# A retention layer and a gated MLP on one core: from scheduled program order to a fixed one, with attention output made transposed and its state kept in PSUM

## The chip, the core and the metric

The kernel runs on one core of a Trainium2 chip. The metric is device time in microseconds (us), as the median of several runs of the whole kernel. Each run also has a span (first to last instruction of the core) and a mean granted clock of TensorE. The engines are named as in the profile: PE (TensorE matmuls), PEld (its weight loads), DVE (VectorE), ACT (ScalarE), POOL (GpSimd) and SP (SyncE, which here issues DMA).

## The reference, cut to what matters

```python
B, H, S, D = 4, 8, 768, 64            # q, k, v: fp32, N(0, 0.1)
for t in range(S):                    # retention: a decaying state per head
    state = gamma * state + outer(k[t], v[t])
    y[t]  = scale * q[t] @ state
x = y as [3072 tokens, 512]
h = x @ w_in                          # w_in  [512, 2048]
g = h * cos(h)
out = g @ w_out                       # w_out [2048, 512]
```

Both kernels compute the recurrence in chunks of 128 tokens (24 chunks, 6 per batch): inside a chunk as masked attention with decay factors folded into q and k (or v), between chunks through the state. The MLP runs on groups of four chunks (512 tokens, six groups). For each group there are 16 "F steps" (four matmuls of 512 columns into one bank, then a sine on ACT and a multiply on DVE) and 64 "O matmuls" for the output. F(g,f) is F step f of group g. Everything that PE reads is bf16, so both weight matrices are cast from fp32 once.

## The kernel before

The parts that the change touches. x is made with tokens on partitions, so each group needs 16 transposes by PE and four DVE copies before its F steps ("T"). The state is summed in fp32 in SBUF by DVE. The program is written chunk by chunk, with MLP units put in by a table.

```python
def load_weights():
    for i in range(KIN):
        ...                                        # whole rows of w_in, 1 MB each
        nc.vector.tensor_copy(out=w_in_sb[:, i, :], in_=st)
    for i in range(KOUT):
        ...
        nc.scalar.copy(out=w_out_sb[:, i, :], in_=st[:, :DM])    # on ACT

def moe_tr_unit(g, i):
    for j in range(GT):
        nc.tensor.transpose(pt[:, ts(j, 128)], x_sb[:, (g * GT + j) % XR, ts(i, 128)], ident)
    nc.vector.tensor_copy(out=xt[:, i, :], in_=pt)

def moe_f_unit(g, f):
    for i in range(KIN):
        nc.tensor.matmul(hp, lhsT=w_in_sb[:, i, ts(f, 128)], rhs=xt[:, i, :], ...)
    nc.scalar.activation(out=cosb, in_=hp, func=AF.Sin, bias=halfpi)
    nc.vector.tensor_tensor(out=gt[:, f, :], in0=hp, in1=cosb, op=ALU.mult)
...
def conv_qk(cc):                                   # decay factors, both on DVE
    nc.vector.tensor_tensor(out=qg[:, co + cc], in0=qf[cc][0], in1=gqbig[:, co + cc], op=ALU.mult)
    nc.vector.tensor_tensor(out=kg[:, co + cc], in0=qf[cc][1], in1=gkbig[:, co + cc], op=ALU.mult)
...
for j in range(2):                                 # state: fp32 add, then a scaled bf16 copy
    nc.vector.tensor_tensor(out=stt[...], in0=stt[...], in1=dps[j][...], op=ALU.add)
for j in range(2):
    nc.vector.tensor_scalar(out=stb[...], in0=stt[...], scalar1=float(scale), ...)
```

Of the kernel before, what the change touches and what calls it, by code (L numbers as in the profile page):

```python
# [13 lines left out]
ALU = mybir.AluOpType  # L14


@with_exitstack
def kernel(
# [9 lines left out]
    nc = tc.nc  # L28
# [6 lines left out]
    NCH = NC // 2  # L35

    scale = 1.0 / math.sqrt(D)
    gammas = [1.0 - 2.0 ** (-5.0 - h) for h in range(H)]

# [5 lines left out]
    XR = 12  # L45

    const = ctx.enter_context(tc.tile_pool(name="const", bufs=1))
    wpool = ctx.enter_context(tc.tile_pool(name="wpool", bufs=1))
    xpool = ctx.enter_context(tc.tile_pool(name="xpool", bufs=1))

    ident = const.tile([128, 128], BF16)
    maskJ = const.tile([128, HP, 128], BF16)
    gqbig = const.tile([128, NC, H, D], BF16)
    gkbig = const.tile([128, NC, H, D], BF16)
    pidx1 = const.tile([128, 1], FP32)
    pidxC = const.tile([128, NC], FP32)
    pidxCn = const.tile([128, NC], FP32)
    halfpi = const.tile([128, 1], FP32)
    def setup_consts_first():
        nc.gpsimd.iota(pidx1, pattern=[[0, 1]], base=1, channel_multiplier=1,  # L60
                       allow_small_or_imprecise_dtypes=True)
        make_identity(nc, ident)

    def setup_consts_early():
        lgbig = wstage.tile([128, 4, H, D], FP32, name="sti")[:, 0]
        for h in range(H):
            nc.vector.memset(lgbig[:, h], math.log(gammas[h]))
        for c in range(NC):
            nc.vector.tensor_scalar(out=pidxC[:, c : c + 1], in0=pidx1,
                                    scalar1=float(128 * c), scalar2=None,  # L70
                                    op0=ALU.add)
        nc.vector.tensor_scalar(out=pidxCn, in0=pidxC, scalar1=-1.0,
                                scalar2=None, op0=ALU.mult)
        for c in range(NC):
            nc.scalar.activation(out=gqbig[:, c], in_=lgbig, func=AF.Exp,
                                 scale=pidxC[:, c : c + 1])
            nc.scalar.activation(out=gkbig[:, c], in_=lgbig, func=AF.Exp,
                                 scale=pidxCn[:, c : c + 1])

    def setup_consts_late():  # L80
        nc.vector.memset(maskJ, float(scale))
        for hp in range(HP):
            nc.gpsimd.affine_select(
                out=maskJ[:, hp], in_=maskJ[:, hp], compare_op=ALU.is_ge,
                fill=0.0, base=0, pattern=[[1, 128]], channel_multiplier=-1,
            )
        nc.gpsimd.memset(halfpi, math.pi / 2.0)

    w_in_sb = wpool.tile([128, KIN, DF], BF16)
    w_out_sb = wpool.tile([128, KOUT, DM], BF16)  # L90
    wstage = ctx.enter_context(tc.tile_pool(name="wstage", bufs=2))

    def load_weights():
        for i in range(KIN):
            st = wstage.tile([128, DF], FP32, name="sti")
            nc.sync.dma_start(out=st, in_=moe_w_in[ts(i, 128), :])  # L96
            nc.vector.tensor_copy(out=w_in_sb[:, i, :], in_=st)
        for i in range(KOUT):
            st = wstage.tile([128, DF], FP32, name="sti")
            nc.sync.dma_start(out=st[:, :DM], in_=moe_w_out[ts(i, 128), :])  # L100
            nc.scalar.copy(out=w_out_sb[:, i, :], in_=st[:, :DM])  # L101

    x_sb = xpool.tile([128, XR, DM], BF16)

    qkv_pool = ctx.enter_context(tc.tile_pool(name="qkv", bufs=2))
    cvt_pool = ctx.enter_context(tc.tile_pool(name="cvt", bufs=2))
    st_pool = ctx.enter_context(tc.tile_pool(name="state", bufs=2))
    tr_pool = ctx.enter_context(tc.tile_pool(name="tr", bufs=2))
    am_pool = ctx.enter_context(tc.tile_pool(name="am", bufs=4))
    xt_pool = ctx.enter_context(tc.tile_pool(name="xt", bufs=2))  # L110
    g_pool = ctx.enter_context(tc.tile_pool(name="g", bufs=2))
    c_pool = ctx.enter_context(tc.tile_pool(name="c", bufs=3))
    o_pool = ctx.enter_context(tc.tile_pool(name="o", bufs=3))

    ps_tr = ctx.enter_context(tc.tile_pool(name="ps_tr", bufs=2, space=bass.MemoryType.PSUM))
    ps_a = ctx.enter_context(tc.tile_pool(name="ps_a", bufs=2, space=bass.MemoryType.PSUM))
    ps_y = ctx.enter_context(tc.tile_pool(name="ps_y", bufs=2, space=bass.MemoryType.PSUM))
    ps_h = ctx.enter_context(tc.tile_pool(name="ps_h", bufs=2, space=bass.MemoryType.PSUM))

    moe_state = {}  # L120

    def moe_tr_unit(g, i):
        if i == 0:
            moe_state["xt", g] = xt_pool.tile([128, KIN, GT * 128], BF16, name="xt")
        xt = moe_state["xt", g]
        pt = ps_tr.tile([128, GT * 128], BF16, name="pt", tag="tr")
        for j in range(GT):
            nc.tensor.transpose(pt[:, ts(j, 128)],
                                x_sb[:, (g * GT + j) % XR, ts(i, 128)], ident)
        nc.vector.tensor_copy(out=xt[:, i, :], in_=pt)  # L130

    def moe_f_unit(g, f):
        if f == 0:
            moe_state["gt", g] = g_pool.tile([128, KOUT, GT * 128], BF16, name="gt")
        xt = moe_state["xt", g]
        gt = moe_state["gt", g]
        hp = ps_h.tile([128, GT * 128], FP32, name="hp")
        for i in range(KIN):
            nc.tensor.matmul(hp, lhsT=w_in_sb[:, i, ts(f, 128)],  # L139
                             rhs=xt[:, i, :],  # L140
                             start=(i == 0), stop=(i == KIN - 1))
        cosb = c_pool.tile([128, GT * 128], BF16, name="cosb")
        nc.scalar.activation(out=cosb, in_=hp, func=AF.Sin, bias=halfpi)  # L143
        nc.vector.tensor_tensor(out=gt[:, f, :], in0=hp, in1=cosb, op=ALU.mult)  # L144

    def moe_o_unit(g, j):
        gt = moe_state["gt", g]
        op = ps_y.tile([128, DM], FP32, name="op", tag="yo")
        for f in range(KOUT):
            nc.tensor.matmul(op, lhsT=gt[:, f, ts(j, 128)],  # L150
                             rhs=w_out_sb[:, f, :],
                             start=(f == 0), stop=(f == KOUT - 1))
        ob = o_pool.tile([128, DM], FP32, name="ob")
        nc.scalar.copy(out=ob, in_=op)  # L154
        nc.gpsimd.dma_start(out=out[ds((g * GT + j) * 128, 128), :], in_=ob)  # L155

    def moe_units_for_group(g):
        for i in range(KIN):
            yield ("T", g, i)
        for f in range(KOUT):  # L160
            yield ("F", g, f)
        for j in range(GT):
            yield ("O", g, j)

    sched = [[] for _ in range(B * NC + 8)]
    for g in range(NG):
        counts = [6, 6, 6, 6] if g < 2 else [4, 4, 4, 4, 2, 2, 2, 2]
        units = list(moe_units_for_group(g))
        pos = 0
        for off, cnt in enumerate(counts):  # L170
            for u in units[pos : pos + cnt]:
                sched[GT * g + 4 + off].append(u)
            pos += cnt
    sched0 = [[] for _ in sched]
    last_t = {}
    for ci, lst in enumerate(sched):
        for u in lst:
            if u[0] == "T":
                last_t[u[1]] = ci
    for ci, lst in enumerate(sched):  # L180
        f = [u for u in lst if u[0] == "F" and last_t[u[1]] < ci][:2]
        sched0[ci] = f
        sched[ci] = [u for u in lst if u not in f]

    def emit_moe0(ci):
        for kind, g, idx in sched0[ci]:
            moe_f_unit(g, idx)

    def emit_moe(ci):
        for kind, g, idx in sched[ci]:  # L190
            if kind == "T":
                moe_tr_unit(g, idx)
            elif kind == "F":
                moe_f_unit(g, idx)
            else:
                moe_o_unit(g, idx)

    def stage_qkv(b, half, v_on_sync=False):
        res = []
        for cc in range(NCH):  # L200
            qf = qkv_pool.tile([128, H, D], FP32, name=f"qf{cc}")
            kf = qkv_pool.tile([128, H, D], FP32, name=f"kf{cc}")
            vf = qkv_pool.tile([128, H, D], FP32, name=f"vf{cc}")
# [9 lines left out]
        return res  # L213

    setup_consts_first()
    pending = [stage_qkv(0, 0, True), stage_qkv(0, 1, True)]
    setup_consts_early()
    setup_consts_late()

# [140 lines left out]
```

## Time and profile before

| | before |
|---|---|
| median of 4 runs | 283.88 us (283.24 to 285.16) |
| span of the profiled run | 278.8 us |
| PE busy | 241.5 us, so PE idle 37.3 us |

First the page of the kernel before. Each digit of the slice rows is the busy share, in tenths, of a fortieth of the span; PEclk is the granted TensorE clock in tenths of full speed. In the last two lines the columns are source line, engine, operation, output and inputs, shapes, count, busy time and mean ns, and then the engine's idle time just before these instructions, with what ended most of it.

```profile
span 278.8 us, 4341 instructions
...
PE 241.5 (87%) x1680; PEld 125.8 (45%) x1680; DVE 167.9 (60%) x324; ACT 143.8 (52%) x222; POOL 55.3 (20%) x82
...
PE   0178868869857999998999999999999999999992
...
PEclk9999999988988999999999999999999999999998
DMA  7999998998997600011000000101001010001011
...
L139 PE MATMUL hp<-xt,w_in_sb 128*128 128x512 bf16 x384 | 100.1, 387 | 4.6 <-DVE gt L144 4.1
...
L150 PE MATMUL op<-w_out_sb,gt 128*128 128x512 bf16 x384 | 90.2, 380 | 5.9 <-ACT w_out_sb L101 5.8
```

The 387 and 380 ns are spans of matmuls that overlap; they are not the rate. For the rate one takes the chain of work that ended last (start, length, what):

```profile
89.81 6.99 PE op L150 x32
```

By the timeline these 32 O matmuls began at 89.73 and ended 7.07 us later. The last one's own span is about 0.38 us, so the 31 steps between starts are (7.07 - 0.38) / 31 = 0.216 us each. The 768 matmuls of F and O at 216 ns are 166 us, the floor of any version that keeps this work at this rate.

The windows view of the same kernel gives busy time by stage (from:to, length, busy us and count of each engine, granted clock, DMA share, GB/s):

```profile
0.00:41.00 41.00, 22.74 (x201) 16.50 (x202) 29.03 (x68) 23.22 (x35) 21.05 (x34) 1.00 1.03 311
41.00:89.00 48.00, 36.74 (x230) 18.19 (x230) 37.35 (x67) 28.67 (x47) 19.83 (x22) 0.93 0.96 290
...
100.00:275.00 175.00, 170.99 (x1172) 85.45 (x1170) 98.41 (x186) 86.42 (x132) 11.33 (x21) 1.00 0.07 29
```

There are two stages. To 89 us the loads bound the kernel (DMA share near 1). From 100 us PE is busy 171 of 175 us and bounds it. The view of waits says what PE stood for (us in total, times, longest):

```profile
PE pq L228 <- DVE qg L248: 14.4, 4, 9.3
PE op L150 <- ACT w_out_sb L101: 5.8, 5, 1.9
```

### The profile page before, as it was taken

The numbers are of one execution on the slowest core, as the hardware profiler recorded it, in microseconds if no ns is written. First come the engines' busy times: TensorE is split into PE (matmuls) and PEld (weight loads), VectorE is DVE, ScalarE is ACT, GpSimd is POOL, SyncE is SP. The second block draws the span as 40 slices with busy tenths as digits, with TensorE's granted clock in tenths as the row PEclk, the third lists the DMA queues.
The fourth block names the chain that finished last, engine by engine and source line by source line (L and its number), as shares of the span: only waits on it lengthen the run. The fifth ranks groups of instructions, "written<-read, shape, count | busy, mean of one in ns | idle before, by whom it ended". The sixth has DMA issues, their size and how long they took to land.

```text
span 278.8 us, 4341 instructions
## 1 busy us (share of the span) xinstructions
PE 241.5 (87%) x1680; PEld 125.8 (45%) x1680; DVE 167.9 (60%) x324; ACT 143.8 (52%) x222; POOL 55.3 (20%) x82
## 2 busy tenths in 40 slices
PE   0178868869857999998999999999999999999992
PEld 0166544434323555444645554545554454444440
DVE  5478799868875179970899873518871345331300
ACT  5964615877544276744376682615753345343410
POOL 8576204542632200011000000000001000001010
PEclk9999999988988999999999999999999999999998
DMA  7999998998997600011000000101001010001011
GB/s 194 330 304 331 394 317 237 299 327 260 319 320 217 190 38 4 0 65 76 12 2 1 2 0 38 40 38 40 1 2 75 0 75 2 38 39 75 2 75 75
DMA packets 39381, 33.84 MB, mean 121 GB/s; under 512 B 32576, under 2 KB 32576, under 8 KB 38848
## 3 DMA queue, kind: packets, MB, share of 16 engines
q1 hardware_dynamic: 34080, 16.26, 20.7%
q0 software_dynamic: 5280, 17.31, 17.5%
q8 instruction: 13, 0.21, 0.3%
q14 instruction: 8, 0.07, 0.1%
HBM read 27.26 MB, written 6.29 MB: 120 GB/s over the span
## 4 chain that ended last, share of the span: by engine, by line
issue 55%; DMA 16%; PE 12%; SPq 5%; POOL 4%; ACT 3%; DVE 3%; POOLq 0%; DVEq 0%; ACTq 0%
DMA sti<-in_moe_w_out_dram 10%; PE hp L139 5%; DMA sti<-in_moe_w_in_dram 4%; POOL out_dram L155 4%; PE op L150 3%; SPq L207 2%; DMA kf_147<-in_k_dram 2%; ACT w_out_sb L101 2%; SPq L210 2%; SPq L96 1%; ACT cosb L143 1%; DVE stb L321 1%; PE pq L228 1%; PE ap L272 1%; ACT sq L231 1%
## 5 line engine op out<-in xcount | busy, mean ns | idle before, releaser
L139 PE MATMUL hp<-xt,w_in_sb 128*128 128x512 bf16 x384 | 100.1, 387 | 4.6 <-DVE gt L144 4.1
L144 DVE TENSOR_TENSOR gt<-hp,cosb 128x512 bf16<-128x512 f32 x96 | 65.5, 687 | 62.8 <-ACT cosb L143 62.0
L150 PE MATMUL op<-w_out_sb,gt 128*128 128x512 bf16 x384 | 90.2, 380 | 5.9 <-ACT w_out_sb L101 5.8
L143 ACT ACTIVATE cosb<-hp,halfpi 128x512 bf16<-128x512 f32 x96 | 65.5, 689 | 39.2 <-PE hp L139 37.5
L150 PEld LDWEIGHTS <-gt 128*128 128x128 bf16 x384 | 36.8, 98 | 48.8 <-issue 6.5
L139 PEld LDWEIGHTS <-w_in_sb 128*128 128x128 bf16 x384 | 35.7, 99 | 42.8 <-issue 11.4
L155 POOL DMA_DIRECT2D out_dram<-ob x24 | 13.0, 542 | 156.8 <-ACT ob L154 156.8
L154 ACT COPY ob<-op 128x512 f32<-128x512 f32 x24 | 14.0, 586 | 53.7 <-PE op L150 53.7
L276 DVE TENSOR_TENSOR amt<-ap,maskJ 128x512 bf16<-128x512 f32 x48 | 32.0, 683 | 9.3 <-PE ap L272 9.0
L231 ACT COPY sq<-pq 128x1024 bf16<-128x1024 bf16 x24 | 24.1, 1011 | 13.1 <-PE pq L229 7.1
L228 PE MATMUL pq<-ident,qg 128*128 128x128 bf16 x96 | 17.3, 245 | 14.4 <-DVE qg L248 14.4
L272 PE MATMUL ap<-sq 64*128 64x128 bf16 x192 | 17.7, 240 | 3.7 <-DVE stt L317 1.8
L297 PE MATMUL yp<-vb,amt 128*128 128x64 bf16 x192 | 19.1, 205 | 1.9 <-DVE amt L276 1.7
L228 PEld LDWEIGHTS <-qg 128*128 128x128 bf16 x96 | 10.3, 110 | 18.2 <-DVE qg L248 15.6
L317 DVE TENSOR_TENSOR stt<-stt,dp 64x256 f32<-64x256 f32 x40 | 16.6, 416 | 2.8 <-PE dp L310 1.7
L297 PEld LDWEIGHTS <-amt 128*128 128x128 bf16 x192 | 14.4, 105 | 7.9 <-DVE amt L276 4.0
L301 ACT CAST x_sb<-yp 128x512 bf16<-128x512 f32 x24 | 14.0, 584 | 7.2 <-PE yp L297 7.2
L229 PE MATMUL pq<-ident,kg 128*128 128x128 bf16 x96 | 17.2, 245 | 0.0
L272 PEld LDWEIGHTS <-sq 64*128 64x128 bf16 x192 | 9.9, 102 | 14.3 <-issue 9.6
L101 ACT CAST w_out_sb<-sti 128x512 bf16<-128x512 f32 x16 | 9.9, 617 | 12.7 <-DMA sti<-in_moe_w_out_dram 12.6
L321 DVE TENSOR_SCALAR stb<-stt 64x256 bf16<-64x256 f32 x40 | 12.2, 306 | 6.8 <-PE yp L290 5.8
L290 PE MATMUL yp<-stb,sq 128*128 128x128 bf16 x80 | 14.8, 236 | 0.5 <-DVE stb L321 0.2
(141 smaller groups left out, 179.7 us busy)
## 6 DMA issues: line engine op xcount, KB each, us to landing
out_dram<-ob POOLq DMA_DIRECT2D x24, 256.0 KB, 2.3
sti<-in_moe_w_in_dram SPq DMA_DIRECT2D x4, 1024.0 KB, 8.8
sti<-in_moe_w_out_dram SPq DMA_DIRECT2D x16, 256.0 KB, 4.1
kf_123<-in_k_dram SPq DMA_DIRECT2D x1, 256.0 KB, 2.7
vf_124<-in_v_dram SPq DMA_DIRECT2D x1, 256.0 KB, 3.4
qf_122<-in_q_dram POOLq DMA_DIRECT2D x1, 256.0 KB, 4.4
kf_129<-in_k_dram SPq DMA_DIRECT2D x1, 256.0 KB, 5.0
vf_130<-in_v_dram SPq DMA_DIRECT2D x1, 256.0 KB, 6.0
```

Of the source, the lines that this page charges most:

```text
L139: nc.tensor.matmul(hp, lhsT=w_in_sb[:, i, ts(f, 128)], rhs=xt[:, i, :], start=(i == 0), stop=(i == KIN - 1))
L143: nc.scalar.activation(out=cosb, in_=hp, func=AF.Sin, bias=halfpi)
L144: nc.vector.tensor_tensor(out=gt[:, f, :], in0=hp, in1=cosb, op=ALU.mult)
L150: nc.tensor.matmul(op, lhsT=gt[:, f, ts(j, 128)], rhs=w_out_sb[:, f, :], start=(f == 0), stop=(f == KOUT - 1))
L155: nc.gpsimd.dma_start(out=out[ds((g * GT + j) * 128, 128), :], in_=ob)
L228: nc.tensor.transpose(pq[:, 0, hp], qg[:, c, 2 * hp : 2 * hp + 2, :], ident)
L229: nc.tensor.transpose(pq[:, 1, hp], kg[:, c, 2 * hp : 2 * hp + 2, :], ident)
L231: nc.scalar.copy(out=sq, in_=pq)
L272: nc.tensor.matmul(ap[:, hp], lhsT=ktr[hp][po : po + 64, :], rhs=qgt[hp][po : po + 64, :], tile_position=(po, 0))
L276: nc.vector.tensor_tensor(out=amt, in0=ap, in1=maskJ, op=ALU.mult)
L297: nc.tensor.matmul(yp[:, h * D : (h + 1) * D], lhsT=amts[j][:, hp], rhs=vb[:, c, h, :], start=(c == 0), stop=True, skip_group_check=True)
L317: nc.vector.tensor_tensor(out=stt[po : po + 64], in0=stt[po : po + 64], in1=dps[j][po : po + 64], op=ALU.add)
```

## The change

The intent is less work on PE and DVE, and a PE that never stops:

- The second attention product is turned round, so that x comes out of PE already transposed. The 96 PE transposes and 24 DVE copies of x go.
- The state stays in one PSUM bank and is accumulated by PE. DVE's 40 fp32 adds go.
- The decay factor of k moves to v. q's and v's multiplies run on POOL with a broadcast factor; DVE only casts k (`ks`).
- w_in comes in column blocks of 512, w_out in blocks of 512 rows. Both are cast in steps of one f, all on DVE. All loads, and the stores of the output, go to SP's queue.
- Every engine keeps the written order (`manual_schedule`). Each of the 16 steps s of a group is one F step, four O matmuls of the group before, and a quarter of the attention of a chunk ahead.

The diff, cut to its core:

```diff
+    ctx.enter_context(tc.manual_schedule())
...
-    def moe_tr_unit(g, i):
-        ...                                   # 4 transposes and a DVE copy
-    ...                                       # pools, unit table, state adds
+    def conv(ci):
+        ...
+        nc.gpsimd.tensor_tensor(out=qs[n], in0=qf[s], in1=bc(gq), op=ALU.mult)
+        nc.vector.tensor_copy(out=ks[n], in_=kf[s])
+        nc.gpsimd.tensor_tensor(out=vout, in0=vf[s]..., in1=gk..., op=ALU.mult)
...
+    def stage_t(ci):                          # needs qs and ks; 8 transposes into one bank
+        for w, src in enumerate((qs[n], ks[n])):
+            for a in range(HP):
+                nc.tensor.transpose(tr[:, w, a, :], src[:, 2 * a : 2 * a + 2, :], ident)
+        nc.scalar.copy(out=sq[ci % 3], in_=tr)
...
+            nc.tensor.matmul(st_ps[:, a, :], lhsT=ks[n][...], rhs=vnat(n, a),
+                             start=(c == 0 and a == 0), stop=True, ...)   # state in PSUM
...
+                nc.tensor.matmul(yp[:, a, :], lhsT=vp[n][:, a, j, :], rhs=am[ci % 2][j][:, a, :], ...)
+        nc.scalar.copy(out=xt[(ci // GT) % 2][:, :, ts(ci % GT, C)], in_=yp)   # x, transposed
...
+    for ci in range(GT):
+        load_chunk(ci)
+    for r in range(4):
+        load_w_in(r)
+    for ci in range(GT, 2 * GT):
+        load_chunk(ci)
...
+    for g in range(NG + 1):
+        for s in range(16):
+            k4, r = divmod(s, 4)
+            if g == 0:
+                cast_w_in(s)                  # DVE
+            if g < NG:
+                unit_f(g, s)                  # PE F, ACT sine, DVE gt
+            if g == 0 and s % 4 == 3:
+                load_w_out(s // 4)
+            if g == 1 and k4 == 0:
+                for f in range(4 * r, 4 * r + 4):
+                    cast_w_out(f)             # DVE
+            if g > 0:
+                unit_o(g - 1, k4, r)          # 4 O matmuls
+            ci = (g + 1) * GT + k4
+            if ci < NT:
+                if r == 0:
+                    conv(ci)
+                    stage_t(ci)
+                elif r == 1:
+                    stage_a(ci)               # PE scores, DVE mask multiplies
+                elif r == 3:
+                    stage_y(ci)
+                    stage_s(ci)               # PE state, DVE copies of it
+                    if ci + GT < NT:
+                        load_chunk(ci + GT)
```

## The prediction

> **What bounds the kernel now.** The busy table gives PE 241.5 of 278.8 us, but matmul spans overlap. In order of time, 32 O matmuls (512 columns) take 7.07 us: 216 ns each. 768 of these are 166 us; attention's 128-column matmuls follow each other at 57 ns. The windows show PE almost full from 100 us to the end. Before that it starves: the chain of waits shows 41 us before the first F matmul (loads of k and w_in), then waits for single w_out tiles until 88 us.
>
> **What changes.** Removed: 96 transposes of x and their DVE copies (24 x 0.42 us), the fp32 state adds (40 x 0.42), DVE's kg multiplies, ACT's vb casts. Moved to POOL: two 512-element multiplies per chunk. All q, k, v loads go to SP's queue. Every engine now keeps the written order, read from the compiled order and its waits. PE's pure work is about 166 + 24 x 1.7 = 207 us, so the intent is a dense PE. But the order places three waits on PE:
>
> 1. Group 0. DVE's order is cast w_in(s), gt(s), cast w_in(s+1), gt(s+1)..., and F(s+1) needs cast(s+1). gt(s) waits for sin(s), which waits for F(s). So no two steps overlap. A step is F 1.03 + sin 0.69 + gt 0.69 + cast about 0.4 (estimate from the 2048-element cast, 1.23) + handovers of 0.03 to 0.05: 2.9 us, where PE needs 0.86. With each chunk's ks copy, sq copy (1.0, ahead of the next sin), two mask multiplies (1.3) and state copies (0.6) in the same chain, four steps take about 13.9 us, the group 55. PE is then busy about a third of the time; idle stretches of 2 us in this trace (at 61.9 and 82.4 us) were followed by F matmuls at 0.43 us instead of 0.216. [...] I add 10 us: 65.
> 2. Group 1, first four steps. O waits for four w_out casts that DVE reaches only after gt of that step: about 4.6 us a step instead of 1.7 to 2.2, some 10 us lost.
> 3. Every later chunk. The transposes wait for DVE's ks copy, queued behind gt: ready about 2.9 us into the step, PE arrives at 1.95. About 1 us. [...] A chunk takes about 10.2 us, not 8.6.
>
> Start: DMA. Row packets of 256 bytes on the SP queue give about 230 GB/s (estimate from the queue table), 1.1 us per tile. Twelve tiles, w_in, then chunk 4's: its k lands near 30 us, and DVE and PE stop there for it.
>
> **Sum.** Start 31.5 + group 0's remainder 62 + group 1 51 + groups 2 to 4 124 + group 5 28 + last O 14 + tail 4.5 = 315 us span, plus 4.6 outside the span (283.4 against 278.8): 320; I shade to 316 us, range 298 to 336. Faster over 2%: 0.04; within: 0.04; slower: 0.92. Nearly all of it is on PE's critical path; ACT, POOL and DMA stay below PE.
>
> **What shows it.** Group 0 from about 31 to 85-95 us with PE idle, released by DVE casts of w_in; PE waiting for w_out casts next; a 1 to 2 us PE wait for ks per chunk; the last 45 us dense. The windows show PE full only after group 4.
>
> **What would make it wrong.** POOL multiplies above 3 us; a clock that stays full in group 0 (about 10 us less); chunk 4 landing by 24 us; casts much shorter than 0.4 us. If group 0 somehow overlapped, about 270 us.

The sum came to 315 us of span and 320 us in all, shaded to 316. A term of the sum is cut, the reason for a longer wait in each later chunk; the figures still hold it: by difference 10.2 - 8.6 - 1.0 = 0.6 us a chunk, or some 7 of the 124 us of groups 2 to 4. The 10 us for the clock in group 0 (55 to 65) are the author's estimate, for which the text has only the slow F matmuls (0.43 us) of the trace of the kernel before.

## The result and the profile after

Ratios, with their 95% intervals, are given. They compare the fast runs of the two kernels, so they are not quite the ratio of the medians that are quoted.

| | before | after |
|---|---|---|
| median of 4 runs | 283.88 us (283.24 to 285.16) | 311.91 us (310.24 to 355.8) |
| fast runs | all | 313.38, 310.24, 310.44 us |
| ratio of fast runs | | 1.0983 (95%: 1.0909 to 1.1057) |

The change made the kernel about 10% slower. One run of the four, the profiled one, took 355.8 us at a mean granted clock of 0.716; even its dense groups ran at 0.73 to 0.75. It counts as slow, and nothing below rests on it; only rival C takes its question from it. What lowered its clock is not known; in the later runs of this kernel and its variants the mean granted clock was between 0.88 and 0.98. A profile of a fast run came with the first experiment, a plain repeat:

> The changed kernel unchanged, because its first profile fell in the slow state. All theories: about 311 us. Theory W (waits laid down by the written order): group 0 lasts from about 31 to 90 us, each w_in cast follows the gt multiply of the step before, F starts right after the cast, and the granted clock is about 0.6 there only; from group 2 on the clock is near 1.0 and each chunk shows one PE wait of about 1 us for the ks copy. Rival D (DMA: all loads on one queue): the DMA share is near 1 to the end of group 0 and PE waits end with a DMA. Rival C [...]: the granted clock is below 0.9 in groups 2 to 5 also in a fast run, and that accounts for the loss.

It took 310.94 us (309.98 to 314.2), against 281.41 us for the kernel before on the same chip: ratio 1.1081 (1.0991 to 1.117). The profiled run is the one of 314.2 us, the longest of the four: its span is 2.5 to 3.4 us above those of the other three, so where profiles are compared below, differences of some 3 us can be noise. Its page, lines as above:

```profile
span 311.6 us, 3908 instructions
...
PE 239.3 (77%) x1480; PEld 120.4 (39%) x1504; DVE 136.9 (44%) x256; ACT 119.7 (38%) x172; POOL 51.3 (16%) x56
...
PE   1672555636647657999889998899988999999995
...
PEclk9998755595557567999999999999999999999999
DMA  9999993263608006146643466434660000000121
...
L227 PE MATMUL bank<-xt,w_in_sb 128*128 128x512 bf16 x363 | 109.2, 424 | 27.5 <-DVE w_in_sb L114 23.7
...
L241 PE MATMUL bank<-w_out_sb,gt 128*128 128x512 bf16 x381 | 98.2, 385 | 7.5 <-DVE w_out_sb L124 7.3
```

Every engine has less to do: DVE fell from 167.9 to 136.9 us, ACT from 143.8 to 119.7, and 176 PE instructions are gone (1680 to 1504; the page counts 1480, as 24 matmul records are missing, 21 of them of F, which hides some 5 us of busy time at most, an estimate of 24 x 0.216). Yet PE's busy time hardly fell (241.5 to 239.3), and its idle time nearly doubled, from 37.3 to 311.6 - 239.3 = 72.3 us. The slice rows say why: from slice 4 to slice 16 PE's digits are 2 to 7, and in most of these slices PEclk is at 5 to 7; F steps there mostly took 1.89 us instead of 1.04.

The windows of this run:

```profile
31.00:60.00 29.00, 15.64 (x74) 7.00 (x76) 11.67 (x21) 6.73 (x9) 8.86 (x9) 0.56 0.68 144
60.00:96.00 36.00, 21.17 (x107) 10.25 (x108) 13.81 (x27) 9.93 (x14) 5.20 (x5) 0.59 0.48 132
96.00:145.00 49.00, 38.15 (x220) 18.17 (x223) 23.12 (x46) 16.88 (x24) 7.52 (x8) 0.82 0.39 81
145.00:186.00 41.00, 37.10 (x257) 19.08 (x260) 21.67 (x38) 19.92 (x29) 8.33 (x8) 1.00 0.49 104
...
266.00:294.00 28.00, 27.46 (x125) 12.50 (x128) 10.38 (x15) 13.05 (x20) 0.00 (x0) 1.00 0.10 38
```

From 31 to 96 us, which is group 0, no engine is near full: PE 37 of 65 us and partly at half clock, DVE 25, ACT 17, DMA share 0.48 to 0.68. Where no resource is full, a chain of waits bounds. The view of waits names its end:

```profile
PE bank L227 <- DVE w_in_sb L114: 23.7, 12, 2.9
PE bank L171 <- DVE ks L156: 16.9, 19, 1.6
PE bank L171 <- POOL qs L155: 15.0, 5, 5.3
PE bank L241 <- DVE w_out_sb L124: 7.3, 4, 1.8
```

The first, second and fourth line are the three waits that the prediction named. The third is mostly the start, where q has to land first; every version below has 10 to 15 us of it.

One step of group 0 in the timeline (start, length, engine, what, idle time before it) shows the chain:

```profile
37.51 1.04 PE L227 MATMUL bank<-xt,w_in_sb 128*128 128x512 bf16 x4 [2.68 <-DVE w_in_sb L114]
...
38.58 0.69 ACT L230 ACTIVATE cosb<-bank,halfpi 128x512 bf16<-128x512 f32 x1 [3.57 <-PE bank L227]
...
39.30 0.69 DVE L231 TENSOR_TENSOR gt<-bank,cosb 128x512 bf16<-128x512 f32 x1 [1.85 <-ACT cosb L230]
39.72 1.04 POOL L158 TENSOR_TENSOR vp<-vf,gk 128x512 bf16<-128x512 f32 x1 [1.37 <-DMA vf<-in_v_dram]
39.91 1.13 DVE L114 CAST w_in_sb<-wst 128x512 bf16<-128x512 f32 x1
...
41.10 1.89 PE L227 MATMUL bank<-xt,w_in_sb 128*128 128x512 bf16 x4 [2.55 <-DVE w_in_sb L114]
```

F, then sine, then gt, then the cast of the next piece of w_in, then the next F: nothing overlaps. The cast doesn't depend on gt at all. It only stands behind it in DVE's order. The last line also shows the half clock: the four matmuls take 1.89 us there instead of 1.04.

The wait of every later chunk looks like this:

```profile
200.07 0.39 PE L171 MATMUL bank<-ident,qs 128*128 128x128 bf16 x4
200.13 0.69 DVE L231 TENSOR_TENSOR gt<-bank,cosb 128x512 bf16<-128x512 f32 x1 [0.71 <-ACT cosb L230]
200.73 0.42 DVE L156 CAST ks<-kf 128x512 bf16<-128x512 f32 x1
...
201.21 0.40 PE L171 MATMUL bank<-ident,ks 128*128 128x128 bf16 x4 [0.75 <-DVE ks L156]
...
202.38 1.04 POOL L155 TENSOR_TENSOR qs<-qf,gq 128x512 bf16<-128x512 f32 x1 [2.69 <-DMA qf<-in_q_dram]
```

Again the cast could have been done long before; it is queued behind gt, and gt waits for the sine of this very step. (The last line, POOL's multiply, matters for a point further down.)

### The profile page after: what moved, and what is told of

The parts are those of the page before. It is cut to its first block, busy times and chain, and to the rows that moved or that the text cites. A ratio compares the mean times of both kernels' runs of the same rounds, so it can differ in the third digit from the quotient of the medians.

```text
span 353.4 us, 3908 instructions
## 1 busy us (share of the span) xinstructions
PE 286.8 (81%) x1480; PEld 134.3 (38%) x1504; DVE 136.9 (39%) x256; ACT 121.3 (34%) x172; POOL 51.5 (15%) x56
## 4 chain that ended last, share of the span: by engine, by line
PE 69%; DVE 10%; ACT 7%; SPq 4%; DMA 4%; issue 3%; another core or an unknown queue 1%; POOL 0%; DVEq 0%; ACTq 0%; POOLq 0%
PE bank_65 L227 6%; PE bank_69 L241 6%; PE bank_68 L227 5%; PE bank_63 L241 5%; PE bank_64 L227 5%; PE bank_67 L241 4%; PE bank_66 L227 4%; PE bank_63 L227 4%; DMA qf_89<-in_q_dram 4%; PE bank_67 L227 4%; PE bank_69 L227 4%; DVE gt_129 L231 4%; SPq L104 3%; PE bank_65 L241 3%; PE bank_64 L241 3%; PE bank_66 L241 3%
## 5 line engine op out<-in xcount | busy, mean ns | idle before, releaser
L227 PEld LDWEIGHTS <-w_in_sb 128*128 128x128 bf16 x384 | 40.6, 115 | 78.5 <-issue 45.6
L241 PEld LDWEIGHTS <-gt_129 128*128 128x128 bf16 x192 | 21.9, 114 | 42.1 <-issue 42.1
L241 PEld LDWEIGHTS <-gt_130 128*128 128x128 bf16 x192 | 21.8, 114 | 32.5 <-issue 32.5
L241 PE MATMUL bank_69<-w_out_sb,gt_129 128*128 128x512 bf16 x63 | 20.8, 464 | 0.1
L227 PE MATMUL bank_66<-xt_127,w_in_sb 128*128 128x512 bf16 x36 | 13.0, 497 | 6.4 <-DVE w_in_sb L114 6.2
L227 PE MATMUL bank_65<-xt_127,w_in_sb 128*128 128x512 bf16 x34 | 11.8, 478 | 6.0 <-DVE w_in_sb L114 5.8
L241 PE MATMUL bank_63<-w_out_sb,gt_130 128*128 128x512 bf16 x48 | 15.4, 467 | 0.0
L241 PE MATMUL bank_64<-w_out_sb,gt_130 128*128 128x512 bf16 x48 | 15.1, 459 | 0.0
L227 PE MATMUL bank_68<-xt_128,w_in_sb 128*128 128x512 bf16 x40 | 14.0, 474 | 1.1 <-ACT xt_128 L220 0.7
L227 PE MATMUL bank_64<-xt_128,w_in_sb 128*128 128x512 bf16 x42 | 13.8, 463 | 0.2
L203 DVE CAST stb_126<-st_ps 64x256 bf16<-64x256 f32 x24 | 10.1, 422 | 8.1 <-PE st_ps L199 7.5
L227 PE MATMUL bank_63<-xt_127,w_in_sb 128*128 128x512 bf16 x26 | 9.8, 512 | 3.4 <-DVE w_in_sb L114 2.8
L241 PE MATMUL bank_63<-w_out_sb,gt_129 128*128 128x512 bf16 x16 | 6.2, 459 | 7.3 <-DVE w_out_sb L124 7.3
L227 PE MATMUL bank_65<-xt_128,w_in_sb 128*128 128x512 bf16 x31 | 11.5, 506 | 0.5 <-ACT xt_128 L220 0.4
L227 PE MATMUL bank_69<-xt_127,w_in_sb 128*128 128x512 bf16 x33 | 11.3, 474 | 0.4 <-issue 0.2
L230 ACT ACTIVATE cosb_133<-bank_66,halfpi 128x512 bf16<-128x512 f32 x8 | 5.5, 687 | 15.4 <-PE bank_66 L227 15.3
L241 PE MATMUL bank_66<-w_out_sb,gt_129 128*128 128x512 bf16 x32 | 10.6, 467 | 0.0
L241 PE MATMUL bank_65<-w_out_sb,gt_129 128*128 128x512 bf16 x32 | 10.6, 466 | 0.0
L241 PE MATMUL bank_67<-w_out_sb,gt_130 128*128 128x512 bf16 x32 | 10.6, 466 | 0.0
L241 PE MATMUL bank_67<-w_out_sb,gt_129 128*128 128x512 bf16 x31 | 10.3, 462 | 0.2
L230 ACT ACTIVATE cosb_132<-bank_65,halfpi 128x512 bf16<-128x512 f32 x8 | 5.5, 687 | 14.2 <-PE bank_65 L227 14.2
L227 PE MATMUL bank_67<-xt_127,w_in_sb 128*128 128x512 bf16 x19 | 7.5, 529 | 3.2 <-DVE w_in_sb L114 2.4
```

The costliest lines, as they stand in the source:

```text
L203: nc.vector.tensor_copy(out=stb[(ci + 1) % 2][ts(j, 64), :, ts(j, 64)], in_=st_ps[ts(j, 64), :, ts(j, 64)])
L227: nc.tensor.matmul(bank, lhsT=w_in_sb[:, i, ts(f, 128)], rhs=xt[g % 2][:, i, :], start=(i == 0), stop=(i == KIN - 1))
L230: nc.scalar.activation(out=cb, in_=bank, func=AF.Sin, bias=halfpi)
L241: nc.tensor.matmul(bank, lhsT=gt[g % 2][:, f, ts(j, 128)], rhs=w_out_sb[:, f, :], start=(f == 0), stop=(f == KOUT - 1))
```

## The experiments

**Theory (the prediction's).** The written order puts three DVE casts (w_in, w_out, ks) behind a gt that comes late, and PE behind each of them. Emitting each cast earlier, with nothing else changed, should give the time back. **Rival D:** DMA, now on one queue with rows of 256 bytes, bounds the first 150 us, and the casts only wait for data. **Rival C:** the granted clock is at fault, which in the first, slow profile was 0.57 from 33 to 110 us and 0.73 to 0.75 after that.

The table has the start of F(0,1) and of the first F step of groups 1 to 5, from the profiled runs; differences of the later columns are the lengths of groups. Experiments on one chip are marked by their job.

| run (job) | F(0,1) | F(1,0) | F(2,0) | F(3,0) | F(4,0) | F(5,0) | span | median, us | ratio to before |
|---|---|---|---|---|---|---|---|---|---|
| after_again (1) | 32.4 | 95.3 | 149.9 | 188.7 | 227.3 | 266.4 | 311.6 | 310.94 | 1.1081 |
| win_ahead (1) | 32.7 | 66.3 | 117.7 | 156.5 | 195.1 | 234.1 | 279.3 | 280.77 | 0.9982 |
| wout_ahead (1) | 32.5 | 98.2 | 141.8 | 180.6 | 219.2 | 258.3 | 303.5 | 304.87 | 1.0863 |
| ks_ahead (1) | 32.4 | 94.6 | 144.7 | 179.8 | 214.7 | 250.1 | 295.2 | 297.13 | 1.0573 |
| warm_fill (2) | 32.6 | 90.1 | 141.3 | 180.2 | 218.8 | 257.8 | 303.0 | 305.5 | 1.0746 |
| chunk4_early (2) | 30.2 | 90.1 | 142.9 | 181.8 | 220.3 | 259.4 | 304.6 | 307.34 | 1.0942 |
| all_three (2) | 32.7 | 61.8 | 98.9 | 134.0 | 168.9 | 204.2 | 249.4 | 251.45 | 0.8921 |
| combined (2) | 28.0 | 63.4 | 102.1 | 137.2 | 172.1 | 207.5 | 252.6 | 253.34 | 0.8982 |
| win_and_ks (3) | 32.7 | 58.5 | 106.9 | 142.1 | 176.9 | 212.3 | 257.5 | 259.27 | 0.9249 |
| combined_late_wout (3) | 29.0 | 53.7 | 101.1 | 136.2 | 171.1 | 206.4 | 252.3 | 253.02 | 0.901 |
| late_wout_dve (3) | 29.1 | 53.4 | 101.6 | 136.8 | 171.6 | 207.0 | 252.2 | 253.21 | 0.8944 |
| all_three_pool_q (4) | 36.3 | 70.3 | 107.8 | 142.9 | 177.8 | 213.2 | 258.7 | 260.09 | 0.9196 |

The four jobs ran on four chips; the kernel before had medians of 281.41, 281.73, 281.61 and 282.49 us in them, so differences between jobs are good to about 1 us. All kernels gave correct results. In late_wout_dve and in warm_fill two of the four runs each count as slow only because they are over 1.5% above the fastest of their kernel, at a mean clock lower by at most 0.011; their ratios are from the two others. The profile of late_wout_dve is of one of the runs that count as slow. In jobs 3 and 4 two of the seven runs of the kernel before count as slow too, and the record calls all three comparisons of job 3 "unclear", although their intervals lie below 1.

### win_ahead: cast w_in three steps ahead

```diff
-            if g == 0:
-                cast_w_in(s)
+            if g == 0 and s == 0:
+                for f in range(3):
+                    cast_w_in(f)
+            if g == 0 and s + 3 < 16:
+                cast_w_in(s + 3)
```

> One edit: the casts of w_in run three steps ahead of the F step that needs them. W: group 0 becomes bound by DVE at about 7 us for four steps in place of 14, so it ends 25 to 33 us earlier, total 278 to 286 us. D: the loads land as before, so less than 5 us. C: no gain, or a smaller one, about 5 us.

Measured: 280.77 us (279.84 to 281.1), ratio 0.9982 (0.9918 to 1.0045); 30.2 us less than after_again on the same chip. Group 0 ended 29.0 us earlier (66.3 instead of 95.3), group 1 became 3.2 us shorter (54.6 to 51.4), and the later groups kept their length. PE's wait for w_in casts fell from 23.7 to 1.4 us, while its wait for ks grew from 16.9 to 19.4:

```profile
PE bank L171 <- DVE ks L156: 19.4, 19, 2.8
...
PE bank L227 <- DVE w_in_sb L114: 1.4, 1, 1.4
```

This one edit puts the changed kernel level with the kernel before. Rival D falls as the cause of group 0's length: the same loads in the same order were there 29 us earlier.

### wout_ahead: cast w_out before the step that needs it

```diff
-            if g == 1 and k4 == 0:
-                for f in range(4 * r, 4 * r + 4):
+            if g == 0 and s in (9, 13):
+                for f in range(4 * ((s - 9) // 4), 4 * ((s - 9) // 4) + 4):
+                    cast_w_out(f)
+            if g == 1 and s in (0, 1):
+                for f in range(8 + 4 * s, 12 + 4 * s):
                     cast_w_out(f)
```

> One edit: w_out is cast before the step that needs it (half in the last steps of group 0, half ahead of the gt multiply in group 1's first two steps). W: the four first steps of group 1 shorten by 8 to 12 us in all, but half of the casts now lengthen group 0's chain by about 1.4 us each four, so the total falls 5 to 9 us, to 302 to 306. D: no change, or slower where DVE waits for the tile. C: no change.

Measured: 304.87 us (304.1 to 307.43), ratio 1.0863; 6.1 us less than after_again. Group 1 went from 54.6 to 43.6 us, so the wait itself was worth 11.0 us, the size that the prediction gave it. But group 0 became 2.9 us longer. Its chain now holds eight w_out casts too (1.42 us for four in an undisturbed place, so 2.8 us), which would explain it, and the whole gained less than the part.

### ks_ahead: copy k one chunk ahead

The copy of chunk ci+1 is emitted in step r == 2 of chunk ci.

```diff
-        nc.vector.tensor_copy(out=ks[n], in_=kf[s])     # in conv
...
+    def conv_k(ci):
+        nc.vector.tensor_copy(out=ks[ci % NB], in_=kf[ci % PRE])
...
                 if r == 0:
                     conv(ci)                 # without the copy of k
+                    if ci == GT:
+                        conv_k(ci)
                     stage_t(ci)
+                elif r == 2:
+                    if ci + 1 < NT:
+                        conv_k(ci + 1)
```

> One edit: ks of a chunk is copied two steps before its transposes, in the chunk before. W: the PE wait at the transposes, about 1 us in each of 16 chunks of groups 1 to 4 and in group 0, goes: 14 to 20 us less, 291 to 297 us. [...] D and C: no change within 2 us.

Measured: 297.13 us (296.26 to 298.47), ratio 1.0573; 13.8 us less than after_again. Groups 2 and 3 went from 38.8 and 38.6 to 35.1 and 34.9 us, 0.9 us a chunk. But group 0 hardly moved (95.3 to 94.6), although four chunks are made in it too. PE's waits there changed their name:

```profile
PE bank L229 <- DVE w_in_sb L114: 30.5, 15, 3.1
```

The wait for ks was gone and the wait for w_in casts grew from 23.7 to 30.5 us. In a serial chain the copy costs the same wherever it stands. So with w_in mended too, this edit could be worth more. The expectation for all three did not allow for that: it added the single gains.

### all_three: the three edits together

> The three edits of win_ahead, wout_ahead and ks_ahead together. If the three waits are separate parts of one chain on PE (W), their gains of 30.2, 6.1 and 13.8 us add: about 261 us; group 0 is now bound by DVE, so half of the w_out casts there cost up to 3 us: 260 to 265. If they hide one another, or a limit beneath them appears (DMA in group 0, which ran at a share near 1.1 to 66 us in win_ahead), 268 us or more.

Measured: 251.45 us (250.06 to 252.9), ratio 0.8921 (0.888 to 0.8963). That is 59.5 us less than after_again, where the single gains add up to 30.2 + 6.1 + 13.8 = 50.1 us, and 10.8% less than the kernel before. It is below both ranges (260 to 265, and 268 or more), so the expectation missed. Its page, two of PE's waits and two of its windows:

```profile
span 249.4 us, 3932 instructions
...
PE 217.5 (87%) x1504; PEld 113.2 (45%) x1504; DVE 136.7 (55%) x256; ACT 119.1 (48%) x172; POOL 51.6 (21%) x56
```

```profile
PE bank L229 <- DVE w_in_sb L114: 1.4, 1, 1.4
...
PE bank L173 <- DVE ks L165: 0.6, 2, 0.4
```

```profile
32.00:62.00 30.00, 22.38 (x181) 12.12 (x180) 26.84 (x53) 16.08 (x23) 11.85 (x11) 0.96 1.11 250
...
134.00:169.00 35.00, 34.55 (x249) 18.14 (x249) 19.78 (x35) 19.25 (x28) 8.45 (x9) 1.00 0.56 121
```

DVE is busy 136.7 us, as in after_again (136.9). The work is the same, only its order differs, and 62.2 us of span are gone: PE's idle time fell from 72.3 to 249.4 - 217.5 = 31.9 us, and its busy time by 21.8 us; 14.4 us of that are in group 0, where the granted clock is now 0.96 instead of 0.56 to 0.59: its windows (31 to 96 us before, 32 to 62 now) hold 181 matmul records each, busy 36.81 and 22.38 us. A group of the middle takes 35 us with PE busy 34.55: from 62 us on PE bounds, as the change intended. In group 0 the DMA share is now 1.11, and DVE is busy 26.84 of 30 us: one of these two has taken over as the bound there. Which of them, the last experiments ask.

### warm_fill: what is the half clock worth?

Five more matmuls, whose result nobody reads, follow each F step of group 0, to keep PE busy. The casts stay where they were.

```diff
             if g < NG:
                 unit_f(g, s)
+            if g == 0:
+                fill(5)          # lhsT=ident, rhs=xt[0][:, 0, :], into a spare bank
```

> The changed kernel with five filler matmuls after each F step of group 0 into a PSUM bank that nothing else uses at that time; they fit into PE's waits, and F and its cast keep their order. It measures what the half clock of group 0 costs by itself. W with the clock as a second cost: the granted clock of 31 to 95 us rises from about 0.57 to above 0.85, F takes 0.86 in place of 1.7 us, and the total falls by 8 to 14 us, to 297 to 303. If the half clock costs nothing (PE waits anyway): same within 2 us, 309 to 313. If the fillers stay cold they only add: 320 or more.

Measured: 305.5 us (301.13 to 306.47), 5.4 us below after_again's median; the profiled spans differ by 8.6 us. The median lies between the two ranges that were expected (297 to 303, and 309 to 313). The ratio, 1.0746 (1.0668 to 1.0824), rests on two runs only. The clock rose to 0.88 from 31 to 60 us and to 1.00 from 60 to 91. A window and two steps of the timeline:

```profile
60.00:91.00 31.00, 22.14 (x150) 10.72 (x148) 14.78 (x27) 9.24 (x13) 5.33 (x5) 1.00 0.57 147
```

```profile
55.27 1.04 PE L227 MATMUL bank<-xt,w_in_sb 128*128 128x512 bf16 x4 [1.71 <-DVE w_in_sb L114]
...
56.14 1.24 PE L238 MATMUL bank<-xt,ident 128*128 128x512 bf16 x5
...
58.15 1.04 PE L227 MATMUL bank<-xt,w_in_sb 128*128 128x512 bf16 x4 [0.76 <-DVE w_in_sb L114]
```

Now every F step from F(0,2) on takes 1.04 us (F(0,1) still took 1.91), and the step from 55.27 to 58.15 is 2.88 us, which is the chain of the prediction without any clock loss (2.9). In after_again a like step, without attention work in it, took 3.72 us (55.40 to 59.12). The difference, 0.84 us, is that of the two F durations (1.89 and 1.04). But group 0 as a whole ends only 5.2 us earlier. In three of four steps the fillers stand in front of attention matmuls, and where they are slow themselves they delay these: in the step F(0,1) they took 2.34 us, its score matmuls began at 36.55 instead of 34.22, and the step went from 5.14 to 6.31 us. So 5.2 us is what is left after the fillers' own cost. An upper estimate for the half clock in F in group 0 is 12 slow F steps (counted in after_again's timeline) x 0.85 = 10.2 us. Between these two it stays open. Group 1, which has no fillers, was 3.4 us shorter too (51.2 instead of 54.6). Either way rival C can't be the main cause: with the clock mended, over 50 of the 60 us that all_three gains are still missing, and in groups 2 to 5 the clock is 1.00 without any help.

### chunk4_early: load chunks 4 to 7 between the blocks of w_in

```diff
     for r in range(4):
         load_w_in(r)
-    for ci in range(GT, 2 * GT):
-        load_chunk(ci)
+        load_chunk(GT + r)
```

> The changed kernel with its first loads in another order: after chunks 0 to 3 the four w_in loads alternate with chunks 4 to 7, in place of all of w_in first. W: PE's first stop in group 0 (to 31.5 us, until chunk 4's q and k have landed) ends near 25 to 27 us, and since group 0 is one chain, all of it moves: 304 to 306 us. If later loads of w_in then come late, less. D (bandwidth bound to the end of group 0): no change.

Measured: 307.34 us (306.24 to 310.6), ratio 1.0942; 3.6 us below after_again, a little less than expected. F(0,1) started at 30.2 instead of 32.4. The landing of chunk 4 is thus a real stop in the start, but most of the gap between F(0,0), at 26, and F(0,1) remained: this step still took 4.1 us.

### combined, win_and_ks, combined_late_wout, late_wout_dve: can all_three be beaten?

"combined" is all_three with the load order of chunk4_early, the odd w_in casts on ACT, and the last two blocks of w_out cast a step later.

> The three edits, the load order of chunk4_early, every second cast of w_in on ACT, and the last two groups of w_out casts one step later than in all_three. W: 4 to 6 us below all_three by the load order, 1 to 4 more by the shared casts, so 250 to 258 us, clearly below the kernel before (281 us in the first job). If DMA bounds group 0, no better than all_three.

Measured: 253.34 us (251.42 to 254.66), ratio 0.8982 (0.8935 to 0.9029). This is within the range for the number, but not below all_three, which was the point. The line that seemed to explain it:

```profile
48.98 1.43 DVE L125 CAST w_out_sb<-wst 128x512 bf16<-128x512 f32 x4 [4.79 <-DMA wst<-in_moe_w_out_dram]
```

The w_out block now lands later, and DVE stood 4.79 us for it in a fixed order, with mask multiplies and gts behind it that were ready: the score matmuls had ended at 43.34, and the mask multiplies ran at 50.33. (That mending this alone did not help, the next runs show.) A cast that is moved ahead of its data blocks an engine as a cast that is too late does.

"win_and_ks" is all_three without the w_out edit. It was to tell whether the 9.4 us (59.5 - 50.1) above the sum come from win and ks hiding behind each other in group 0.

> The edits of win_ahead and ks_ahead together, w_out untouched. It asks why all_three gained 59 us where the single gains sum to 50. If the ks wait in group 0 was hidden behind the wait for the w_in cast (ks_ahead alone left group 0's end at 94.6 against 95.3 us, while win_ahead shows ks waits of up to 2.8 us there), the two together end group 0 near 60 us, not 66, and the total is 258 to 262 us. If their gains only add: 266 to 268 us, and the surplus lay with the w_out edit.

Measured: 259.27 us (258.54 to 262.42), ratio 0.9249; 22.3 us below the kernel before of its job, where win_ahead was 0.6 below and after_again 29.5 above. So the two edits together took off 29.5 + 22.3 = 51.9 us, where apart they took 30.2 and 13.8, in sum 44.0. The extra 7.9 us are in group 0: it ended at 58.5, against 66.3 with win_ahead alone. That is the hidden wait of ks_ahead, found again. These sums cross two chips by way of the kernel before, whose medians differ by 0.2 us.

"combined_late_wout" is combined with every w_out block cast one step (the first block two steps) before the O matmuls that need it; "late_wout_dve" is the same with all w_in casts on DVE.

```diff
-            if g == 0 and s in (9, 13):
...
-            if g == 1 and s in (1, 2):
...
+            if (g, s) in ((0, 14), (1, 0), (1, 1), (1, 2)):
+                r0 = 0 if g == 0 else s + 1
+                for f in range(4 * r0, 4 * r0 + 4):
                     cast_w_out(f)
```

> The kernel of the run combined, with the w_out casts moved later: group r is cast one step ahead of the O step that needs it (last steps of group 0, first three of group 1). In combined DVE stood 4.8 us for a w_out tile at 49 us, with the gt multiplies queued behind it. If that is what ate the gain of the load order, this gives 244 to 249 us, below all_three. If the loads bound group 0 in any order: 250 to 254.

> The same, with all w_in casts on DVE. If DVE bounds group 0 once the order is mended, 2 to 5 us slower than combined_late_wout; if DMA or PE does, the same within 1 us.

Measured: 253.02 us (252.2 to 254.36) and 253.21 us (249.8 to 253.82); ratios 0.901 (0.8942 to 0.9078) and 0.8944 (0.8813 to 0.9075). Group 0 ended at 53.7 and 53.4, 8 us before all_three's, and group 1 lost all of it again. The lines are of combined_late_wout:

```profile
PE bank L243 <- DVE w_out_sb L125: 8.5, 3, 5.1
```

```profile
DVE w_out_sb L125 <- DMA wst<-in_moe_w_out_dram: 7.4, 2, 4.2
```

The casts waited for their data. In every order tried, group 2 begins at 98.9 us or later. Whether ACT helps with the casts makes a difference of 0.2 us in the medians (the two fast runs of late_wout_dve are 249.8 and 252.81, so 1 or 2 us in DVE's favour are not excluded). So DVE's load is not the limit there. That the loads are is argued, not shown: the DMA share of combined_late_wout is 1.08 to 1.10 from 20 to 63 us, and DVE waits for w_out, but no run changed the bytes or their rate with the order kept.

### all_three_pool_q: is it the queue that makes the loads slow?

In all_three, the rows of 256 bytes on SP's queue moved at 217 to 221 GB/s from 5 to 16 us, and w_in, in rows of 2048 bytes, at 371 to 394 GB/s from 17.5 to 26 us. The kernel before, with two queues and wider rows of w_in, had 311 GB/s in 41 us. So the last run loads the q tiles of chunks 4 to 23 through POOL's queue, as the kernel before did.

```diff
+            if t is qf and GT <= ci < 2 * GT:
+                continue
+            eng = nc.gpsimd if t is qf and ci >= 2 * GT else nc.sync
+            eng.dma_start(out=t[s], in_=...)
...
+            if ci in (1, 2):                  # q of chunks 4 to 7, in POOL's order
+                load_q_pool(2 * ci + 2)
+                load_q_pool(2 * ci + 3)
```

> all_three with one thing changed: the q tiles of chunks 4 to 23 are loaded by POOL's queue, as in the kernel before, and no longer by SP's. In all_three the rows of 256 bytes on SP's queue moved at 217 to 225 GB/s by the view of transfers, the weights at 390, and the DMA share was 1.1 to 63 us; the kernel before, with its two queues, moved 311 GB/s in its first 41 us. Theory (the rate of SP's small packets bounds the first 63 us): a higher rate in 15 to 60 us, POOL waits less for q tiles, group 2 starts 3 to 6 us before all_three's 98.9, total 246 to 249 us (ratio 0.873 to 0.885). Rival (what bounds is the bytes themselves, or POOL's issue time of 0.88 us per load comes into its multiplies' way): group 2 starts at 98 to 102, total 250 to 256 (ratio 0.888 to 0.91).

Measured: 260.09 us (258.82 to 260.36), ratio 0.9196 (0.913 to 0.9263): worse than all_three's 0.8921, and above both ranges (246 to 249, and 250 to 256). The rate did not rise: 259 GB/s over the first 70 us, against 255 in all_three. What changed was the order of arrival. POOL issued the q loads of chunks 4 to 7 at 11 and 15 us, where they shared the DMA engines with the first chunks and w_in, and these came later: the median w_in block landed 15.1 us after its issue instead of 9.8, F(0,0) moved from 25.9 to 27.6, and chunk 4's k, still behind w_in in SP's queue, let F(0,1) start at 36.3 instead of 32.7. PE's longest wait for ks was 7.0 us. From there on group 0 was 5 us longer as well (34.0 instead of 29.2). POOL also spent 0.9 us on each issue (1.95 us for the pair at 11.2 us), between its multiplies; how much of the loss is this, and how much the order of arrival, the run doesn't separate. The theory that the queue alone sets the rate falls in this form. A version that keeps the order of arrival and changes only the queue was not tried, so what could raise the rate of the small rows stays open.

## Why the prediction was right

The prediction gave 316 us (298 to 336), with 0.92 for slower. The fast runs were at 310.24 to 313.38 us, and the repeat's median at 310.94. Point by point:

- **What bounds the kernel before.** Loads and waits for weights to 89 us, then PE. That stands, by the windows. No run tested whether less work for DVE and ACT would by itself have helped the kernel before.
- **The chain of group 0**, the main term, was right in mechanism and size. A step was put at 2.9 us; without a clock loss (warm_fill) the steps F(0,6), F(0,7), F(0,10) and F(0,14) measured 2.87 to 2.88. Four steps with a chunk's attention were put at 13.9 us; from F(0,4) on they took 14.0, 14.6 and 14.6 there, fillers included. The start plus group 0 was put at 31.5 + 62 = 93.5 us; F(1,0) came at 95.3. Undoing it alone gave 30.2 us.
- **"I add 10 us" for the half clock.** That the clock falls and F slows is shown: F took 1.89 us instead of 1.04, at a mean granted clock of 0.56 to 0.59 from 31 to 96 us, where PE was busy 37 of 65 us and its waits for DVE mostly lasted 1.5 to 2.9 us. In warm_fill, with PE busy 22 of 31 us and waits of 0.5 to 1.7 us, the clock stayed at 1.00 from 60 to 91 us. How the clock depends on the waits was not shown beyond this. The size in group 0 lies between some 5.2 us (net of the fillers' cost) and an estimate of 10.2, so the 10, the author's estimate, is at the upper end.
- **Group 1's w_out casts, "some 10 us".** Right: moving them shortened group 1 by 11.0 us. The prediction put the whole group at 51 us; it took 54.6.
- **The ks wait, about 1 us a chunk.** Right: mean 16.9 / 19 = 0.89 us by the view of waits, and 0.9 us a chunk gained when it was moved.
- **"A chunk takes about 10.2 us."** This is the term that was mis-sized. Groups 2 to 4 were put at 124 us and took 266.4 - 149.9 = 116.5, a chunk 9.7. The addition of some 0.6 us a chunk makes some 7 us over 12 chunks, about the whole error. In the trace above, a ks copy ends at 201.15 us, while POOL's next multiply starts only at 202.38, when its q has landed. In groups 2 to 4 none of the 12 ks copies ran beside a POOL multiply; each took 0.42 us. Elsewhere DVE's casts did take longer beside one: the w_in cast at 39.91 in the step shown from group 0 began while POOL's multiply (39.72 to 40.76) ran, ended at 41.04, 0.28 us after it, and took 1.13 us where an undisturbed one takes 0.42. Of the 56 casts of w_in, w_out and ks in after_again, seven were delayed so: each started while a POOL multiply ran, ended 0.28 us after it, and took 0.48 to 1.26 us. The other 49 took 0.41 to 0.43. What delays them was not shown. Only one of the seven is a ks copy after group 0 (at 122.02, in group 1), so in the later chunks such a delay came once.
- **POOL's multiplies.** The risk that they take over 3 us did not come true. In after_again they took 1.04 us (qs) and 1.05 us (vp) in the mean.
- **Outside the span.** 4.6 us were added, after_again has 314.2 - 311.6 = 2.6.

The sum, 319.6, was 5.4 us above the profiled run's 314.2 before it was shaded to 316: groups 2 to 4 (+7.5), all that follows them in the span (+1.3) and this last term (+2.0), against group 1 (-3.6) and the start with group 0 (-1.8). That these errors partly cancel, and that the shading, for which no reason was given, went the right way, is luck; that the main terms fit is not. The prediction also said that nearly all of it was on PE's critical path, and all_three shows that: with no work removed, the mended order took 59.5 us off.

The prediction had put the ks copy into group 0's chain. The expectation for all_three, made later, added the three gains as if they were independent, and saw no way to a time below their sum. In group 0 they are not: ks and w_in stand in one chain, and taking away one lengthens the wait for the other. Of a mended order the prediction said only that with group 0 overlapped the kernel would take about 270 us; win_ahead, which does that, took 280.77. With all three waits mended PE is the bound from 62 us on, and the same computation ends at 251 us, 30 us below the kernel before.

## What to carry to other kernels

When you fix the program order, the order in which you emit an instruction is a dependency, even where the data has none (here moving the w_in casts alone took 30.2 us off): list for each engine what stands directly in front of what the next engine waits for, and emit casts and copies as soon as their inputs are there, one to three steps ahead, but not before their data lands. If no engine and no DMA is near full in a window, look there for a serial chain, and expect that mending one of its links shows up as a longer wait at the next (in ks_ahead the wait for w_in casts grew from 23.7 to 30.5 us). A rewrite that comes out slower may be one reordering away from a gain: here three casts emitted earlier turned 10% slower into 11% faster.
